# Reordering the loads and folds of the start, and the softmax sums of four slots, in a sparse-attention plus feed-forward kernel

## The chip, the cores and the metric

The kernel runs on one core of a Trainium2 chip. The metric is the device time of one execution in microseconds (us). The core has five engines that run side by side, each with its own instruction queue worked in order: PE (TensorE, matrix products and transposes), DVE (VectorE), ACT (ScalarE), POOL (GpSimd) and SP (SyncE, which here only issues DMAs). POOL issues DMAs as well; its transfers can convert fp32 to fp16 on the way. All transfers share 16 DMA engines.

## The reference

For 8 batches of 8 heads, 576 positions and head size 64, attention is computed under a sparse mask; heads 0 to 3 see the last 32 positions, heads 4 to 7 see the earlier positions with the same remainder modulo 32. The result, 4608 tokens of 512 features, goes through a multiplicative feed-forward layer.

```python
mask_local = (rel >= 0) & (rel < stride)
mask_strided = (rel >= 0) & (pos[None, :] % stride == pos[:, None] % stride)
...
scores = scores - np.max(scores, axis=-1, keepdims=True)
attn = np.exp(scores)
attn = attn / (np.sum(attn, axis=-1, keepdims=True) + 1e-09)
return np.matmul(attn, v).astype(np.float32)
...
a = x @ w1
b = x @ w2
h = a * b @ w3
return (h @ w_out).astype(np.float32)
```

Here w1 and w2 are 512x1024, w3 is 1024x1024 and w_out is 1024x512.

## The kernel before

The attention is cut into 32 pairs of heads, four to a batch: pairs 0 and 1 of a batch are local, 2 and 3 strided. Pair i goes through these steps, each a function:

- `load_qk(i)`: POOL issues the loads of q and k as fp16 into a tile `s16` (four buffers): two DMAs for a local pair, four for a strided one.
- `load_v(i, gate)`: SP issues the loads of v in fp32, three DMAs of 256-byte rows for a local pair (tile `vst`, two buffers) or six for a strided one (tile `vsS`). With `gate` DVE first writes a few zeros into the tile, so that the loads start only when DVE has reached that point in its queue.
- `emit_T`: PE transposes q and k; DVE or ACT copy them out as `qT` and `kT`.
- `emit_S`: PE computes the scores; DVE adds the mask (`tmp`, L312).
- `emit_max` (DVE, L320), `emit_sub` (DVE, L327), `emit_exp` (ACT, L339).
- `emit_norm`: DVE sums a row (`sm`, L347), takes the reciprocal (`rc`, L349), POOL multiplies (L350).
- `emit_cast_v`: v becomes fp16 (`vh`, L260), on POOL, or on ACT for pair 0.
- `emit_P`: PE transposes the probabilities (`pp`), ACT copies them out (`pT`).
- `emit_V`: PE multiplies with v; ACT, and for a strided pair DVE too, write the result into `xT`, the input of the feed-forward layer.

The two last weight matrices are first folded into one: the product of w3 and w_out is computed in eight parts. `fold_t(mc, eng)` transposes a part of w3 on PE (`w3tp`) and copies it out (`w3T`) with DVE (`cp`) or ACT (`act`); `fold_m(mc)` is eight 512-column matrix products with w_out (`fps`, L222) and a copy by ACT (`wfh`, L224). `load_w3(g)` loads the quarter of w3 that folds 2g and 2g+1 take; `load_wo` loads w_out and `load_w12(half)` half of the columns of w1 and w2; all are POOL's.

The feed-forward layer runs in pieces: `emit_a` (four 512-column products `aps`, a copy `asb` by ACT), `emit_b` (four products `bps`, a multiplication `abt` by DVE, L244) and `emit_out` (eight products `ops` with the folded weights, a copy `osb` by ACT, a store by SP). `feed(us, batches)` emits the next pieces in their order until their nominal time, 0.87 us for an a or b piece and twice that for an out piece, has used up a credit; it takes only tokens of the first `batches` batches, so the first piece needs all four pairs of batch 0.

The order is written out by hand: instructions enter each engine's queue in the order of the calls. Loads, folds and the pairs 0 to 4 come one by one (L444 to L537). Then come four slots, n = 5 to 8 (L540 to L561), each with the scores of pair n, the normalisation of pair n-1, the transposes of pair n+1 and some pieces, and then slots n from 9 on with another fixed order (L562 to L590). A strided pair's tiles `vsS`, `qTS` and `prS` exist twice, so pairs use them in turn.

Of the kernel before, what the change touches and what calls it, by code (L numbers as in the profile page):

```python
# [27 lines left out]
def kernel(  # L28
# [49 lines left out]
    def load_qk(i):  # L78

        b, hp, local, par = where(i)  # L80
        h0 = 2 * hp
        t = ld.tile([P, 2, ST * D], FP16, tag="s16", bufs=4, name="s16")
        if i + 1 == 4 * B:
            for p0 in (0, HALF):
                nc.vector.memset(t[p0 + 32:p0 + HALF, :, (ST - 1) * D:ST * D], 0.0)
        for src, p0 in ((q, 0), (k, HALF)):
            if local:
                nc.gpsimd.dma_start(t[p0:p0 + HALF, :, 0:LB * D],
                                    src[b, h0:h0 + 2].rearrange("h (p j) d -> p h (j d)", j=LB))
            elif i + 1 == 4 * B:  # L90
                for r in range(3):
                    n = ST if r < 2 else ST - 1
                    nc.gpsimd.dma_start(t[p0 + NA * r:p0 + NA * r + NA, :, 0:n * D],
                                        _ap(src[b, h0], 11 * r * D,
                                            [[NR * D, NA], [S * D, 2], [1, n * D]]))
            else:
                for h in range(2):
                    nc.gpsimd.dma_start(t[p0:p0 + SW, h, :],  # L98
                                        _ap(src[b, h0 + h], 0,
                                            [[11 * D, 3], [NR * D, NA], [1, ST * D]]))  # L100
        cast[i] = t

    def load_v(i, gate=False):

        b, hp, local, par = where(i)
        h0 = 2 * hp
        if local:
            vt = ld.tile([LW, LB, 2, D], FP32, tag="vL", name="vst")
            if gate:
                nc.vector.memset(vt[:, 0:2, :, 0:1], 0.0)  # L110
            nc.sync.dma_start(vt[:, 0], v[b, h0:h0 + 2, 0:LW].rearrange("h p d -> p h d"))
            for h in range(2):
                nc.sync.dma_start(vt[:, 1:LB, h, :],
                                  _ap(v[b, h0 + h], 32 * D,
                                      [[D, LW], [HALF * D, LB - 1], [1, D]]))
        else:
            vt = vsS[par]
            if gate:
                nc.vector.memset(vt[:, :, 0:1], 0.0)
            for r in range(3):  # L120
                for half in range(2):
                    n = 6 if half == 0 else 5 if r < 2 else 4
                    p0 = HALF * half + NA * r
                    nc.sync.dma_start(vt[p0:p0 + NA, :, 0:n * D],
                                      _ap(v[b, h0], (11 * r + 6 * half) * D,
                                          [[NR * D, NA], [S * D, 2], [1, n * D]]))
        staged[i] = vt
# [70 lines left out]
    def load_w3(g):  # L198
        w3 = wst.tile([P, 2, DF], FP16, tag="w3s", bufs=4, name="w3s")
        nc.gpsimd.dma_start(w3, w3r[:, 2 * g:2 * g + 2, :])  # L200
        for i in range(2):
            w3st[2 * g + i] = w3[:, i, :]
# [5 lines left out]
    def fold_t(mc, eng=nc.vector.tensor_copy):  # L208

        w3 = w3st.pop(mc)  # L210
        tp = psF.tile([P, KC2, P], FP16, tag="f", name="w3tp")
        for kc in range(KC2):
            nc.tensor.transpose(tp[:, kc, :], w3[:, kc * P:(kc + 1) * P], id16)
        w3T = wst.tile([P, KC2, P], FP16, tag="w3T", name="w3T")
        eng(out=w3T, in_=tp)
        aqs[mc] = w3T

    def fold_m(mc):
        w3T = aqs.pop(mc)
        ps = psF.tile([P, DM], FP32, tag="f", name="fps")  # L220
        for kc in range(KC2):
            nc.tensor.matmul(ps, w3T[:, kc, :], woh[:, kc, :], start=(kc == 0),  # L222
                             stop=(kc == KC2 - 1))
        nc.scalar.copy(out=wfh[:, mc, :], in_=ps)  # L224
# [31 lines left out]
    def emit_cast_v(i, eng=nc.gpsimd.tensor_copy):  # L256
        b, hp, local, par = where(i)
        vst = staged.pop(i)
        vh = att.tile(list(vst.shape), FP16, tag="vhL" if local else "vhS", name="vh")
        eng(out=vh, in_=vst)  # L260
        pts[i] = [vh if local else vh.rearrange("p h (t d) -> p t h d", d=D)]
# [180 lines left out]
    cp, act = nc.vector.tensor_copy, nc.scalar.copy  # L442
    with tc.manual_schedule():
        load_qk(0)  # L444
        load_v(0)
        make_identity(nc, id16)
        load_wo()
        make_maskL()
        load_w3(0)
        load_qk(1)  # L450
        load_w3(1)
        for t in qTS + prS:
            nc.vector.memset(t, 0.0)
        make_sel()
        load_qk(2)
        emit_T(0)
        emit_S(0)
        emit_max(0)
        load_v(1, True)
        emit_sub(0)  # L460
        make_maskS()
        emit_exp(0)
        emit_cast_v(0, act)
        for t in vsS:
            nc.vector.memset(t, 0.0)
        load_v(2)
        load_v(3)
        emit_norm(0)
        load_w3(2)
        load_qk(3)  # L470
        load_w3(3)
        load_qk(4)

        fold_t(0, cp)
        emit_T(1)
        fold_t(1, act)
        fold_m(0)
        emit_S(1)
        emit_max(1)
        emit_P(0)  # L480
        emit_sub(1)
        fold_m(1)
        emit_exp(1)
        emit_V(0)
        fold_t(2, cp)
        emit_T(2)
        emit_norm(1)
        fold_m(2)
        emit_S(2)
        emit_max(2)  # L490
        load_w12(0)
        emit_cast_v(1)
        load_qk(5)
        fold_t(3, act)
        emit_sub(2)
        emit_exp(2)
        fold_m(3)
        emit_T(3)
        fold_t(4, act)
        emit_P(1)  # L500
        emit_S(3)
        emit_max(3)
        emit_cast_v(2)
        load_w12(1)
        fold_m(4)
        emit_norm(2)
        emit_sub(3)
        emit_V(1)
        fold_t(5, cp)
        emit_exp(3)  # L510
        fold_t(6, act)
        emit_P(2)
        emit_norm(3)
        emit_cast_v(3)
        load_v(4, True)
        load_qk(6)
        load_qk(7)
        load_qk(8)
        fold_m(5)
        emit_V(2)  # L520
        emit_P(3)
        fold_m(6)
        emit_V(3)
        emit_T(4)
        fold_t(7, cp)
        feed(0.8, 1)
        emit_S(4)
        emit_max(4)
        fold_m(7)
        load_v(5, True)  # L530
        emit_sub(4)
        emit_exp(4)
        load_v(6, True)
        load_v(7)
        feed(1.6, 1)
        emit_T(5)
        feed(1.6, 1)  # L537

        f = 3.6
        for n in range(5, 9):  # L540
            emit_S(n)
            feed(0.15 * f, 1)
            emit_max(n)
            if n > 5:
                emit_V(n - 2)
            feed(0.25 * f, 1)
            emit_norm(n - 1)
            emit_cast_v(n - 1)
            load_qk(n + 4)
            if n > 5:  # L550
                load_v(n + 2)
            emit_sub(n)
            emit_exp(n)
            emit_T(n + 1)
            feed(0.6 * f, 1)
            emit_P(n - 1)
            if n == 8:
                emit_norm(n)
                for i in (8, 9):
                    emit_cast_v(i)  # L560
                load_v(11)  # L561
        for n in range(9, NP + 2):  # L562
            full = (n - 1) // 4
            first = full - 1 if n % 4 == 1 else full
            f = 5.2
            if n + 4 < NP:
                load_qk(n + 4)
            if n + 3 < NP:
                load_v(n + 3)
            if n < NP:  # L570
                emit_S(n)
            emit_V(n - 2)
            if n + 1 < NP:
                emit_T(n + 1)
            feed(0.1 * f, first)
            if n < NP:
                emit_max(n)
            feed(0.15 * f, first)
            if n < NP:
                emit_sub(n)  # L580
                emit_exp(n)
            feed(0.15 * f, full)
            if n <= NP:
                emit_P(n - 1)
            feed(0.2 * f, full)
            if n < NP:
                emit_norm(n)
                if n + 1 < NP:
                    emit_cast_v(n + 1)
            feed(0.4 * f, full)  # L590
        feed(1e9, B)
# [31 lines left out]
```

## Time and profile before

The times are 297.69, 298.36 and 299.65 us, median 298.36. The profiled execution took 297.85 us, of which its span, from the first to the last instruction, is 296.1; 1.75 us lie around it.

| engine | busy us | share of the span | instructions |
|---|---|---|---|
| PE (matrix products) | 268.4 | 91% | 3793 |
| DVE | 192.6 | 65% | 334 |
| ACT | 169.0 | 57% | 297 |
| POOL | 145.9 | 49% | 187 |

HBM is read with 41.43 MB and written with 9.44 MB. On the chain of work that ended last PE has 71% of the span, DVE 10%, ACT 5%, DMA 5%, POOL 4%. Busy time is time in which an engine had an instruction running; matrix products are pipelined, so a busy PE need not be at its peak. "Idle before, releaser" in a row is how long the engine had waited and for whom. Rows of a timeline give start, duration, engine, source line, operation, what it writes and reads, and the idle time before it.

### The profile page before, as it was taken

To read this page: it belongs to the slowest core of one execution; us is meant where nothing else is said; L and a number is where in the kernel's file an instruction comes from. 1 tells how busy PE (TensorE), PEld (TensorE's weight loads), DVE (VectorE), ACT (ScalarE), POOL (GpSimd) and SP (SyncE) were. 2 spreads that over 40 slices of the span, in tenths; PEclk is the share of its full clock that TensorE was granted. 3 is DMA by queue.
4 is the path that set the end of the run, shared out by engine and by line. 5 is a ranking of instruction groups with operands and counts; after the bars stand their busy time and mean duration, and the time that the engine had idled before them with its cause. 6 is when DMAs were issued, how large, how long until landed. Compare 5 with 4: busy or idle time off the path is not lost.

```text
span 296.1 us, 9087 instructions
## 1 busy us (share of the span) xinstructions
PE 268.4 (91%) x3793; PEld 143.6 (48%) x3793; DVE 192.6 (65%) x334; ACT 169.0 (57%) x297; POOL 145.9 (49%) x187
## 2 busy tenths in 40 slices
PE   1179889689799999999999999999999999999994
PEld 0145455345445555555555555555556544444441
DVE  1838647865888778887879787778877870332210
ACT  3326675366656766675676567667667644333322
POOL 8664974368767636873584566456724410000000
PEclk9999999999979999999999999999999999999999
DMA  7999999866689649765965687668613002000113
GB/s 133 187 203 212 192 205 183 158 116 102 143 182 202 101 84 210 124 103 151 194 98 83 181 169 104 117 159 156 122 41 110 2 2 106 35 2 35 71 43 135
DMA packets 65545, 36.70 MB, mean 124 GB/s; under 512 B 45792, under 2 KB 59872, under 8 KB 65504
## 3 DMA queue, kind: packets, MB, share of 16 engines
q0 software_dynamic: 27584, 14.88, 35.9%
q1 hardware_dynamic: 37920, 21.24, 26.7%
q8 instruction: 29, 0.48, 0.7%
q14 instruction: 12, 0.10, 0.1%
HBM read 41.43 MB, written 9.44 MB: 172 GB/s over the span
## 4 chain that ended last, share of the span: by engine, by line
PE 71%; DVE 10%; ACT 5%; DMA 5%; POOL 4%; issue 2%; SPq 1%; DVEq 0%; POOLq 0%; ACTq 0%
PE bps L241 19%; PE ops L249 18%; PE aps L231 17%; PE fps L222 4%; PE sp L306 4%; DMA s<-in_k_dram 4%; DVE tmp L312 3%; DVE mx L320 2%; PE pp L362 2%; PE tpq L272 2%; DVE tmp L327 2%; PE pp L367 2%; PE op L382 2%; DMA vsS<-in_v_dram 2%; ACT pT L363 1%
## 5 line engine op out<-in xcount | busy, mean ns | idle before, releaser
L244 DVE TENSOR_TENSOR abt<-bps,asb 128x512 f16<-128x512 f32 x72 | 49.6, 690 | 39.5 <-PE bps L241 35.2
L241 PE MATMUL bps<-xT,w2h 128*128 128x512 f16 x288 | 74.1, 380 | 0.0
L231 PE MATMUL aps<-xT,w1h 128*128 128x512 f16 x288 | 74.0, 379 | 0.0
L249 PE MATMUL ops<-wfh,abt 128*128 128x512 f16 x288 | 68.3, 386 | 0.0
L235 ACT COPY asb<-aps 128x512 f32<-128x512 f32 x72 | 41.8, 589 | 30.0 <-PE aps L231 29.8
L350 POOL TENSOR_TENSOR pr<-pr,rc 128x864 f16<-128x864 f16 x16 | 27.0, 1690 | 53.4 <-DVE rc L349 29.2
L249 PEld LDWEIGHTS <-abt 128*128 128x128 f16 x288 | 27.5, 99 | 31.5 <-issue 1.6
L252 ACT COPY osb<-ops 128x512 f32<-128x512 f32 x36 | 21.1, 587 | 37.4 <-PE ops L249 34.8
L241 PEld LDWEIGHTS <-w2h 128*128 128x128 f16 x288 | 26.5, 98 | 30.1
L231 PEld LDWEIGHTS <-w1h 128*128 128x128 f16 x288 | 26.9, 98 | 28.3
L350 POOL TENSOR_TENSOR prS<-prS,rc 128x594 f16<-128x594 f16 x16 | 20.1, 1257 | 32.0 <-DVE rc L349 12.1
L327 DVE TENSOR_TENSOR tmp<-tmp,mx 128x864 f32<-128x864 f32 (+1 forms) x32 | 30.6, 957 | 0.9
L320 DVE TENSOR_REDUCE mx<-tmp 128x9 f32<-128x864 f32 (+1 forms) x32 | 29.0, 906 | 0.3
L347 DVE TENSOR_REDUCE sm<-pr 128x9 f32<-128x864 f16 x16 | 16.8, 1049 | 12.8 <-ACT pr L339 12.8
L312 DVE TENSOR_TENSOR tmp<-sp,maskL 128x480 f32<-128x480 f32 (+1 forms) x32 | 18.0, 603 | 9.8 <-PE sp L306 8.9
L339 ACT ACTIVATE pr<-tmp 128x864 f16<-128x864 f32 x16 | 14.8, 923 | 15.9 <-DVE tmp L327 15.1
L272 PE MATMUL tpq<-id,s 54*64 54x54 f16 (+1 forms) x640 | 17.8, 195 | 5.4 <-POOL maskL L140 5.4
L98 POOL DMA_DIRECT2D s<-in_k_dram x30 | 18.0, 612 | 7.0 <-DMA w2h<-in_moe_w_dram 2.7
L272 PEld LDWEIGHTS <-s 54*64 54x64 f16 (+1 forms) x1280 | 14.7, 109 | 10.5 <-DMA s<-in_q_dram 6.5
L272 PE MATMUL tpk<-id,s 54*64 54x54 f16 (+1 forms) x640 | 17.8, 196 | 1.6 <-DMA s<-in_k_dram 1.6
L98 POOL DMA_DIRECT2D s<-in_q_dram x30 | 19.1, 645 | 0.0
L363 ACT COPY pT<-pp 96x640 f16<-96x640 f16 (+1 forms) x32 | 18.6, 630 | 0.6 <-PE pp L362 0.6
(70 smaller groups left out, 334.3 us busy)
## 6 DMA issues: line engine op xcount, KB each, us to landing
out_dram<-osb SPq DMA_DIRECT2D x36, 256.0 KB
vst<-in_v_dram SPq DMA_DIRECT2D x32, 192.0 KB
vsS<-in_v_dram SPq DMA_DIRECT2D x48, 54.0 KB
s<-in_q_dram POOLq DMA_DIRECT2D x16, 144.0 KB, 4.3
s<-in_k_dram POOLq DMA_DIRECT2D x16, 144.0 KB, 5.4
s<-in_q_dram POOLq DMA_DIRECT2D x30, 74.2 KB, 5.8
s<-in_k_dram POOLq DMA_DIRECT2D x30, 74.2 KB, 6.2
w3s<-in_moe_w_dram POOLq DMA_DIRECT2D x4, 512.0 KB, 10.7
```

What stands on the lines that cost most here:

```text
L98: nc.gpsimd.dma_start(t[p0:p0 + SW, h, :], _ap(src[b, h0 + h], 0, [[11 * D, 3], [NR * D, NA], [1, ST * D]]))
L231: nc.tensor.matmul(aps, w1h[:, ci, jc * P:(jc + 1) * P], xT[ci][:, c * NT:(c + 1) * NT], start=(ci == 0), stop=(ci == KC1 - 1))
L235: nc.scalar.copy(out=asb, in_=aps)
L241: nc.tensor.matmul(bps, w2h[:, ci, jc * P:(jc + 1) * P], xT[ci][:, c * NT:(c + 1) * NT], start=(ci == 0), stop=(ci == KC1 - 1))
L244: nc.vector.tensor_mul(abts[c][:, jc, :], bps, abts.pop((c, jc)))
L249: nc.tensor.matmul(ps, abts[c][:, jc, ts * P:(ts + 1) * P], wfh[:, jc, :], start=(jc == 0), stop=(jc == KC2 - 1))
L272: nc.tensor.transpose(tp[HALF * h:HALF * h + HALF, s, :], s16[p0:p0 + npar, h, s * D:(s + 1) * D], id16[p0:p0 + npar, p0:p0 + npar])
L312: nc.vector.tensor_tensor(out=tmp[:, t0:t1, :], in0=sp, in1=msk, op=ALU.add)
L320: nc.vector.tensor_reduce(out=mx, in_=tmp, axis=AX.X, op=ALU.max)
L327: nc.vector.tensor_tensor(out=tmp, in0=tmp, in1=_sub(mx, 0, P, 0, [[1, nt], [0, w]]), op=ALU.subtract)
L350: nc.gpsimd.tensor_tensor(out=prv, in0=prv, in1=_sub(rc, 0, P, 0, [[1, nt], [0, w]]), op=ALU.mult)
L363: nc.scalar.copy(out=pT[:, t0:t1, :], in_=pp)
```

## The change

Only the order of calls changes; no function and no amount of work does.

- Loads of v. Pair 0's load was the second step of the program; now it stands after the maximum of pair 0, gated, where pair 1's stood. Pair 1's moves after the maximum of pair 1, and those of pairs 2 and 3, which stood ungated after the exponential of pair 0, after the maximum of pair 2, both gated.
- Pair 0's v is cast by ACT after the second `fold_t` and no longer right behind the exponential of pair 0.
- Loads of POOL. The first half of w1 and w2 moves ahead of the last quarter of w3. Pair 4's q and k go behind the cast of pair 1, pair 5's and the second half of w1 and w2 behind the normalisation of pair 2.
- `fold_t(6)` moves behind `emit_P(3)`, `fold_m(6)` behind `emit_V(3)`; the first feed-forward piece now precedes `emit_T(4)`, and the second and third pieces stand elsewhere between the steps of pair 4.
- In slots 5 to 8 the sum, reciprocal and normalisation of pair n-1, its cast of v and a load of q and k move ahead of the first piece and of the maximum of pair n; `emit_V(n - 2)` moves behind the second call of `feed`.

```diff
         load_qk(0)
-        load_v(0)
...
         emit_max(0)
-        load_v(1, True)
+        load_v(0, True)
...
         emit_exp(0)
-        emit_cast_v(0, act)
...
-        load_v(2)
-        load_v(3)
         emit_norm(0)
         load_w3(2)
         load_qk(3)
+        load_w12(0)
         load_w3(3)
-        load_qk(4)
 
         fold_t(0, cp)
         emit_T(1)
         fold_t(1, act)
+        emit_cast_v(0, act)
         fold_m(0)
         emit_S(1)
         emit_max(1)
+        load_v(1, True)
         emit_P(0)
...
         emit_max(2)
-        load_w12(0)
+        load_v(2, True)
+        load_v(3, True)
         emit_cast_v(1)
-        load_qk(5)
+        load_qk(4)
...
         emit_cast_v(2)
-        load_w12(1)
         fold_m(4)
         emit_norm(2)
+        load_qk(5)
+        load_w12(1)
         emit_sub(3)
         emit_V(1)
         fold_t(5, cp)
         emit_exp(3)
-        fold_t(6, act)
         emit_P(2)
         emit_norm(3)
         emit_cast_v(3)
...
         emit_V(2)
         emit_P(3)
+        fold_t(6, act)
+        emit_V(3)
         fold_m(6)
-        emit_V(3)
-        emit_T(4)
         fold_t(7, cp)
         feed(0.8, 1)
+        emit_T(4)
+        fold_m(7)
         emit_S(4)
         emit_max(4)
-        fold_m(7)
+        feed(0.8, 1)
         load_v(5, True)
         emit_sub(4)
         emit_exp(4)
         load_v(6, True)
         load_v(7)
-        feed(1.6, 1)
+        feed(0.8, 1)
         emit_T(5)
         feed(1.6, 1)
...
         for n in range(5, 9):
             emit_S(n)
-            feed(0.15 * f, 1)
-            emit_max(n)
-            if n > 5:
-                emit_V(n - 2)
-            feed(0.25 * f, 1)
             emit_norm(n - 1)
             emit_cast_v(n - 1)
             load_qk(n + 4)
+            feed(0.15 * f, 1)
+            emit_max(n)
+            feed(0.25 * f, 1)
             if n > 5:
+                emit_V(n - 2)
                 load_v(n + 2)
             emit_sub(n)
             emit_exp(n)
```

## The prediction

> **What bounds the kernel now.** I read the busy times by stretch first, then what PE waited for, then the timeline where those waits lie. Stretches (start and end, length, then busy us of PE, its weight loads, DVE, ACT, POOL; granted clock, DMA share, GB/s):
>
> ```profile
> 16.00:24.00 8.00, 6.99 (x91) 4.52 (x92) 2.82 (x5) 3.07 (x5) 5.44 (x7) 1.00 1.18 207
> 24.00:32.00 8.00, 6.52 (x120) 3.62 (x118) 6.90 (x10) 4.60 (x8) 4.78 (x7) 1.00 1.10 200
> ...
> 56.00:64.00 8.00, 5.67 (x110) 3.04 (x109) 5.83 (x11) 4.41 (x8) 4.54 (x4) 1.00 0.54 116
> ...
> 80.00:88.00 8.00, 7.26 (x115) 4.05 (x115) 6.40 (x10) 4.76 (x9) 6.52 (x8) 0.79 0.78 174
> 88.00:120.00 32.00, 32.00 (x546) 17.72 (x544) 25.47 (x46) 22.01 (x42) 19.06 (x23) 1.00 0.78 157
> ```
>
> From 88 us on PE never rests and the order is unchanged, so whatever is won or lost by then stays to the end. Until about 56 us the DMA engines are full (share above 1); from 56 to 82 PE idles though DMA is not full. What PE waited for between 16 and 90 us (sum, times, longest):
>
> ```profile
> PE w3tp L213 <- DMA w3s<-in_moe_w_dram: 3.8, 1, 3.8
> PE pp L362 <- POOL pr L350: 3.6, 2, 2.3
> PE op L395 <- ACT pT L370: 1.2, 2, 0.6
> PE fps L222 <- ACT w3T L215: 1.2, 1, 1.2
> ```
>
> The second and third rows lie in slots 5 to 8. One of these waits in the timeline (slot 6; start, duration, engine):
>
> ```profile
> 60.35 0.84 DVE L312 TENSOR_TENSOR tmp<-sp,maskS 128x324 f32<-128x324 f32 x2 [1.61 <-PE sp L306]
> 61.55 0.69 DVE L244 TENSOR_TENSOR abt<-bps,asb 128x512 f16<-128x512 f32 x1 [0.35 <-PE bps L241]
> 62.15 0.76 DVE L320 TENSOR_REDUCE mx<-tmp 128x11 f32<-128x594 f32 x1
> 62.83 1.04 DVE L347 TENSOR_REDUCE sm<-pr 128x9 f32<-128x864 f16 x1
> ...
> 64.35 1.97 POOL L350 TENSOR_TENSOR pr<-pr,rc 128x864 f16<-128x864 f16 x1 [2.80 <-DVE rc L349]
> ...
> 66.37 0.70 PE L362 MATMUL pp<-id,pr 128*96 128x128 f16 x9 [1.26 <-POOL pr L350]
> ```
>
> The sum of pair 5 stands behind a piece's multiplication and the maximum of pair 6, though its exponential ended at 58.8. The loop sum, POOL, transpose, scores, mask, sum takes 7.06 us (the transposes of pairs 4 and 5 start at 59.31 and 66.37).
>
> **Sums first (slots 5 to 8).** The sum can start when `tmp` ends, at 61.2 and not 62.83: 1.6 us off the loop. What limits next: PE's own work in a slot is scores 0.5, transposes 0.5 and 0.65, the product with v 0.42 and about 4.1 pieces of 0.87, 5.65 us together. DVE's is, in slot 5 with local pairs, 1.12 + 1.05 + 0.25 + 2 x 0.69 + 1.05 + 1.06 + 0.46 = 6.4; in slot 6, where pair 6 is strided, about 5.5. The maximum now waits behind sum and reciprocal (1.3), so the exponential comes 1.3 later; its next reader, the sum of the following slot, starts about 2 us after it now (58.8 to 61.2), so this is covered, barely in slot 6. I take 5.45, 6.05, 5.5 and 5.5 us for the slots: 22.5 between the scores of pairs 5 and 9, which now stand at 52.28 and 80.62, 28.34 apart. Gain 5.8; at least 0 if DVE becomes the loop, at most 6.3 (all PE's idle from 56 to 80, 2.33 + 1.26 + 1.52, and 1.2 of the waits for `pT`). The later product with v costs PE nothing: a piece stands in its place while ACT copies `pT`.
>
> **The clock.** In 79.0 to 82.4 PE runs only transposes and small products, and the next eight 512-column products run at half clock:
>
> ```profile
> 79.00:82.40 3.40, 1.81 (x91) 1.55 (x90) 2.58 (x5) 2.91 (x6) 3.40 (x5) 1.00 0.75 179
> 82.40:85.90 3.50, 3.50 (x25) 1.33 (x18) 3.47 (x5) 0.98 (x2) 3.50 (x4) 0.51 0.85 206
> ```
>
> They take 3.53 us where the eight before took 1.90. With the slots closed up that gap falls to about 2.4 us, shorter than any that led to half clock here: gain 1.65 (0 if it comes anyway).
>
> **The start.** Without pair 0's v the first loads are alone. Pair 0's q (issued at 1.34) and k landed at 5.38 and 6.72; a q issued at 60.31 among little traffic landed 3.43 us later. So k of pair 0 lands near 5.6 and all behind it 1.1 us earlier: the first w3 quarter at 15.4 instead of 16.49, pair 1's k at 17.1 instead of 18.19. (Bounds 0 and 1.9, the time that v's packets took, 31 us over 16 engines.) The scores of pair 0 gain nearly nothing: ACT copies kT only behind the mask, at 7.5.
>
> **Pair 0's v.** It now starts where pair 1's did, about 11.1. Pair 1's, issued from 11.29, landed at 25.2 by its completion events: while POOL's loads were queued, the packets of the two queues went one for one (1,103 and 1,112 between 18.5 and 22.0), and v has 1,728. With POOL's queue 1.1 us ahead I take 24.4; the lower bound is 18, by the 6.9 us from 60.38 to 67.2 with little beside. ACT waits for it in front of `wfh`, `pT` of pair 0 and the exponential of pair 1. Its queue: cast 1.14 to 25.6, `wfh` 0.59, `pT` 1.17 to 27.3. `fold_m(1)` ends on PE at 24.0 (25.1 less 1.1); the product with v of pair 0 ends at 27.5 instead of 25.5: 2.0 late, a PE gap of 2.7.
>
> **Pairs 1 to 3.** Pair 1's v, issued at 23.7 behind its maximum, gets the same one-for-one share and lands near 34; POOL waits for it (free at 31.8), and behind its cast stand pair 4's loads, the cast of pair 2 and the normalisation of pair 2. Pair 2's v is issued from 32.7 to 34.8 and follows it through SP's rings: near 39 (the DMAs of a strided v took 6 us under load before, and 3 us free). Cast 0.82, multiplication 1.5: 41.4, where it ended at 39.16. Then, new in this place, four issues on POOL (two of 0.61, two of 0.78: 2.8 us) before pair 3 is normalised: 45.4 instead of 41.3. The last transpose of batch 0 starts at 45.45 instead of 41.69.
>
> **Folds and first piece.** `fold_t(6)` fills the wait for `pT`. But its copy follows `pT` on ACT (0.8, then 1.0), so `fold_m(6)` runs from 47.85 to 49.6; with `fold_t(7)` the first piece is at 50.15, now 44.95. Moving w1/w2's half forward brings nothing: it lands at 41.0 already, before the first piece can run. Moving the last w3 quarter back costs nothing: 34.5 becomes about 40, and its fold is due at 46. The same holds for what POOL issues later: pair 4's loads (from 35) land near 42 and are due at 51, pair 5's near 46, due at 55, the second half of w1/w2 (from 42.6) near 51, due with the ninth piece after 60. The added gate writes are 0.06 us each on DVE. The shuffled pieces around pair 4 are neutral: same work on PE. From there to the scores of pair 5 it is 7.33 us now (with the transposes of pair 4 ahead): 57.6 instead of 52.28, **5.3 late**; POOL's six loads are done by 53, before the sum of pair 4.
>
> **Sum.** +5.3 - 5.8 - 1.65 = -2.15 against 297.85 (span 296.1 and 1.75 around it). For half clock in the new gaps (next) I add 0.8, one time in two of 1.65: -1.35, 296.5. The median of the runs lies 0.5 above the profiled one: **297.0**.
>
> **A rule against it.** The rows say that 3.4 us with hardly a 512-column product are followed by half clock. The change makes two such gaps at the start: 24.0 to 28.9 and 43.6 to 47.85, 4.9 and 4.2 us. Both followed by it costs 3.3 instead of 0.8. The Trainium skill, page "TensorE: Matmul & The Clock Gate" (Part 1), says that the clock halves after an idle window of 3413 ns whose phase runs free of the kernel; the records here agree with the length, 3.41 us, and by it a 4.9 us gap would hold a whole window less than half of the time.
>
> **Rivals.**
> 1. *Loads of v land sooner* than I take, near the unloaded bounds (nothing else of SP's is queued with them). For: unloaded v lands in 2 to 7 us. Against: POOL's ring is full until 40. Then ACT and POOL don't wait; POOL's 2.8 us of issues and the fold behind `pT` remain, the scores of pair 5 are 2.0 late: 2.0 - 5.8 - 1.65 = -5.45, 292.9 as a median.
> 2. *Both gaps at half clock*: -2.15 + 3.3 = +1.15, 299.5.
> 3. *Slower: POOL behind pair 2's v.* If it takes from 32.7 as long as pair 4's, issued at 40.09 and landed at 51.66, it lands at 44.3, 5 us later, and everything to the first piece shifts by that: -1.35 + 5 = +3.65, 302.0. It decides from a landing of about 41.5 on.
>
> That the early half of w1/w2 does nothing is in the forecast already.
>
> **Chances.** Forecast 0.40 (a fifth of it below 295.4), rival 1 0.26, rival 2 0.10, rival 3 0.24. A measurement can tell about 1% (3 us) from no change. Faster 0.26 + 0.08 = 0.34; within 1% 0.32 + 0.10 = 0.42; slower 0.24. Range 292.5 to 302.5 takes in both ends; the likeliest case alone has 295 to 299.
>
> **What would show it.** Right: a PE gap near 24 to 27 released by ACT; `fps` of fold 6 behind a POOL wait near 45; scores of pair 5 near 57 and of pair 9 near 79.5; no half clock near 82. Wrong: first piece before 47 (rival 1), pair 2's cast after 42 (rival 3), or slots that still take 7 us with DVE releasing PE.

## The result and the profile after

The changed kernel took 306.61 us (median of four runs, 305.01 to 307.69) against 299.0 us for the kernel before on the same chip (median of four): a ratio of 1.027, 95% interval 1.022 to 1.031. The change makes the kernel 2.7% slower. The profiled execution after took 305.01 us, its span is 303.3; before it was 297.85 and 296.1, so the two profiles differ by 7.2 us. The page's head and engine totals after:

```profile
span 303.3 us, 9092 instructions
PE 270.3 (89%) x3793; PEld 144.9 (48%) x3793; DVE 192.8 (64%) x337; ACT 168.1 (55%) x297; POOL 145.4 (48%) x187
```

PE has the same 3793 instructions and 1.9 us more busy time (268.4 before); the other 5.3 us are idle time. Where it lies is read from the start of each pair's scores on PE (L306), of the first feed-forward piece (L231) and of the transposes of pair 2's and pair 3's probabilities (L367). Each row is a stretch between two such starts, so the last column can be added up:

| stretch on PE | before, us | after, us | predicted | measured |
|---|---|---|---|---|
| start to the scores of pair 3 | 34.43 | 36.75 | +2.0 | +2.32 |
| to the transposes of pair 2's probabilities | 4.79 | 5.96 | +0.24 | +1.17 |
| to those of pair 3 | 2.47 | 3.92 | +1.52 | +1.45 |
| to the first piece | 3.26 | 4.76 | +1.44 | +1.50 |
| to the scores of pair 5 | 7.33 | 10.05 | +0.1 | +2.72 |
| four slots, to the scores of pair 9 | 28.34 | 27.96 | -5.8 | -0.38 |
| to the scores of pair 10 | 9.31 | 7.67 | -1.65 | -1.64 |
| new half clock, as an allowance | | | +0.8 | in the rows above |
| sum | | | -1.35 | +7.14 |

From the scores of pair 10 to the end both profiles run alike: every later start is 7.14 us later. The busy times by stretch, with the columns as before (length; busy us of PE, weight loads, DVE, ACT, POOL; granted clock, DMA share, GB/s):

```profile
16.00:24.00 8.00, 7.44 (x86) 4.42 (x87) 1.95 (x3) 1.65 (x2) 5.92 (x8) 1.00 1.19 206
...
40.00:48.00 8.00, 5.43 (x58) 3.11 (x59) 2.60 (x7) 3.53 (x7) 8.00 (x12) 0.79 0.87 149
...
80.00:88.00 8.00, 6.95 (x105) 3.40 (x104) 5.42 (x10) 4.57 (x8) 5.14 (x7) 1.00 0.71 135
88.00:120.00 32.00, 30.47 (x542) 17.32 (x542) 25.95 (x46) 22.59 (x41) 20.84 (x25) 1.00 0.73 154
```

The low granted clock has left the row from 80 to 88 (0.79 before, 1.00 now) and stands in the row from 40 to 48, where POOL is busy throughout. What stands ahead of half clock before, a gap with transposes and small products alone, is still there, now near 88 us, but the clock stays at 1.00:

```profile
88.40:92.00 3.60, 2.47 (x94) 1.88 (x94) 3.32 (x8) 3.11 (x6) 2.94 (x4) 1.00 0.90 192
```

From 87.31 to 91.29, 3.98 us, PE has no 512-column product (3.36 us before, from 79.16 to 82.52), and yet the next eight, from 91.29 on, take 1.90 us. In 88 to 120, where PE never rested before, it now lacks 1.5 us: the last slots end later. What PE waited for from 16 to 98 us (sum, times, longest):

```profile
...
PE pp L367 <- POOL prS L350: 2.4, 2, 2.2
PE sp L306 <- ACT kT L281: 2.2, 1, 2.2
PE pp L367 <- ACT qT L281: 1.9, 2, 1.6
...
PE pp L362 <- DVE qTS L285: 1.6, 2, 1.3
PE pp L362 <- ACT kT L286: 1.3, 2, 0.7
```

The largest row of the slots before, `pp` behind POOL's `pr` (3.6 us), is gone. In its place stand rows of about the same sum whose releasers are the copies `qT`, `qTS` and `kT` of the next pair (1.9 less 0.9 that was there before, 1.6 and 1.3). Slot 5 shows why (start, duration, engine, source line):

```profile
64.43 1.63 POOL L350 TENSOR_TENSOR pr<-pr,rc 128x864 f16<-128x864 f16 x1 [6.47 <-DMA vsS<-in_v_dram]
...
65.85 1.12 DVE L327 TENSOR_TENSOR tmp<-tmp,mx 128x864 f32<-128x864 f32 x1
...
66.89 0.45 DVE L285 COPY qTS<-tpq 128x594 f16<-128x594 f16 x1
67.06 0.92 ACT L339 ACTIVATE pr<-tmp 128x864 f16<-128x864 f32 x1 [2.60 <-DVE tmp L327]
...
67.40 0.44 PE L362 MATMUL pp<-id,pr 128*96 128x128 f16 x5 [1.26 <-DVE qTS L285]
67.89 0.64 ACT L286 COPY kT<-tpk 128x594 f16<-128x594 f16 x1
...
68.58 0.38 PE L362 MATMUL pp<-id,pr 128*96 128x128 f16 x4 [0.74 <-ACT kT L286]
68.89 0.53 PE L306 MATMUL sp<-kT,qTS 64*64 64x54 f16 x22
```

POOL's multiplication, which PE used to wait for, is done at 66.06. Yet the transposes of `pr` start at 67.40 and their second half at 68.58. They write into the same two PSUM buffers (PSUM is the memory that PE writes into; the pool `psA` has two buffers) as `tpq` and `tpk`, the transposes of the next pair, and these come free when DVE has copied `qTS` and ACT has copied `kT`. Those copies stand behind the subtraction and the exponential of pair 5 in their engines' queues. The scores of pair 6 read both copies. Before, the same chain ran in slot 5, at the same pace:

```profile
57.00 2.25 POOL L350 TENSOR_TENSOR pr<-pr,rc 128x864 f16<-128x864 f16 x1 [5.34 <-DMA vsS<-in_v_dram]
...
58.69 0.64 ACT L286 COPY kT<-tpk 128x594 f16<-128x594 f16 x1
...
59.31 0.70 PE L362 MATMUL pp<-id,pr 128*96 128x128 f16 x9 [2.33 <-POOL pr L350]
```

There `pr` ended at 59.25 and `kT` at 59.33: two paths of equal length, of which the waits name one. From the scores to the exponential it was 52.28 to 57.86, 5.58 us; now it is 61.44 to 67.06, 5.62. The sum and the reciprocal were ahead of the subtraction already; exchanging them with the maximum moves nothing behind the subtraction.

At the start, POOL's queue (start, duration) shows the chain that delays pairs 2 and 3:

```profile
38.32 1.14 POOL L260 CAST vh<-vst 96x1152 f16<-96x1152 f32 x1 [5.87 <-DMA vst<-in_v_dram]
...
41.47 1.19 POOL L350 TENSOR_TENSOR prS<-prS,rc 128x594 f16<-128x594 f16 x1
...
45.35 1.22 POOL L350 TENSOR_TENSOR prS<-prS,rc 128x594 f16<-128x594 f16 x1
```

POOL stood 5.87 us for the v of pair 1, landed at 38.17; the v of pair 2, at 39.50, was no longer waited for. And PE's queue there:

```profile
42.71 0.51 PE L367 MATMUL pp<-id,prS 128*128 128x128 f16 x6 [2.17 <-POOL prS L350]
43.06 2.88 PE L222 MATMUL fps<-woh,w3T 128*128 128x512 f16 x8
...
46.63 0.77 PE L367 MATMUL pp<-id,prS 128*128 128x128 f16 x6 [0.24 <-POOL prS L350]
```

Fold 5 took 2.88 us here and 1.89 before: it lies in a stretch of half clock.

### The profile page after: what moved, and what is told of

It is laid out like the page before. It is cut to its first block, busy times and chain, and to the rows that moved or that the text cites. A ratio compares the mean times of both kernels' runs of the same rounds, so it can differ in the third digit from the quotient of the medians.

```text
span 303.3 us, 9092 instructions
## 1 busy us (share of the span) xinstructions
PE 270.3 (89%) x3793; PEld 144.9 (48%) x3793; DVE 192.8 (64%) x337; ACT 168.1 (55%) x297; POOL 145.4 (48%) x187
## 4 chain that ended last, share of the span: by engine, by line
PE 67%; DVE 13%; ACT 8%; DMA 4%; POOL 3%; issue 3%; SPq 0%; POOLq 0%; ACTq 0%; DVEq 0%
PE bps L241 18%; PE ops L249 17%; PE aps L231 17%; DMA vst<-in_v_dram 4%; PE sp L306 4%; DVE tmp L312 3%; DVE mx L320 3%; DVE tmp L327 3%; PE fps L222 2%; PE tpq L272 2%; PE pp L362 2%; ACT pT L363 2%; PE op L382 2%; PE pp L367 2%; ACT pr L339 1%
## 5 line engine op out<-in xcount | busy, mean ns | idle before, releaser
L231 PE MATMUL aps<-xT,w1h 128*128 128x512 f16 x288 | 74.0, 379 | 0.0
L249 PE MATMUL ops<-wfh,abt 128*128 128x512 f16 x288 | 66.8, 380 | 0.0
L350 POOL TENSOR_TENSOR pr<-pr,rc 128x864 f16<-128x864 f16 x16 | 26.0, 1625 | 58.2 <-DVE rc L349 32.8
L231 PEld LDWEIGHTS <-w1h 128*128 128x128 f16 x288 | 27.1, 98 | 28.7
L350 POOL TENSOR_TENSOR prS<-prS,rc 128x594 f16<-128x594 f16 x16 | 18.9, 1180 | 29.4 <-ACT asb L235 13.1
L260 POOL CAST vh<-vst 96x1152 f16<-96x1152 f32 x15 | 18.3, 1225 | 5.9 <-DMA vst<-in_v_dram 5.9
L222 PE MATMUL fps<-woh,w3T 128*128 128x512 f16 x64 | 17.9, 430 | 2.1 <-ACT w3T L215 1.7
```

Of the source, the lines that this page charges most:

```text
L231: nc.tensor.matmul(aps, w1h[:, ci, jc * P:(jc + 1) * P], xT[ci][:, c * NT:(c + 1) * NT], start=(ci == 0), stop=(ci == KC1 - 1))
L249: nc.tensor.matmul(ps, abts[c][:, jc, ts * P:(ts + 1) * P], wfh[:, jc, :], start=(jc == 0), stop=(jc == KC2 - 1))
L350: nc.gpsimd.tensor_tensor(out=prv, in0=prv, in1=_sub(rc, 0, P, 0, [[1, nt], [0, w]]), op=ALU.mult)
```

## The experiments

The theory after this reading: (a) the slots gain nothing because the copies of the next pair's q and k are a second path of the same length; (b) the fold that was between the scores of pair 4 and the pieces was a cover, and taking it away costs about 2.2 us; (c) the loads of v, held back, cost the rest through ACT (pair 0) and POOL (pairs 1 and 2), with POOL's new issues. The rivals are named in each expectation. Times are medians, ratios are against the kernel before on the same chip in the same set. One caution for the profiles: with identical code ahead of it, the scores of pair 5 start at 52.04 to 53.70 us in the profiles of before and of the four kernels that change the slots alone. The spread is there at the scores of pair 3 already: 34.19 to 35.86 in six profiles with the old start. So stretches inside one profile are compared, and whole times by their medians.

### The slots

**The new slots alone, on the kernel before.** (In the cuts of the slots some lines are joined by semicolons.)

```diff
         for n in range(5, 9):
             emit_S(n)
-            feed(0.15 * f, 1); emit_max(n)
-            if n > 5: emit_V(n - 2)
-            feed(0.25 * f, 1)
             emit_norm(n - 1); emit_cast_v(n - 1); load_qk(n + 4)
-            if n > 5: load_v(n + 2)
+            feed(0.15 * f, 1); emit_max(n); feed(0.25 * f, 1)
+            if n > 5: emit_V(n - 2); load_v(n + 2)
```

> The kernel before with the new slots 5 to 8 alone. Theory (copies): the next scores wait for the copies of the next pair's q and k, which stand on DVE behind the subtraction and on ACT behind the exponential; before and after, mask, maximum, sum, reciprocal and subtraction all stand ahead of them, only sum and maximum are swapped. Then the scores of pairs 5 to 9 keep their distance of 28.3 us (27.5 to 28.5) and the time is that of before within 1 us; half clock near 82 may or may not stay (1.6 us). Rival (the prediction): 22.5 us between these scores and 5 to 7 us less in time, and then the loss of 7.6 us must come from a start that alone costs 13.

Measured: 296.85 us against 298.05, ratio 0.994 (0.990 to 0.997). The four slots take 27.98 us, as in the whole change, and the half clock after them is gone (granted clock 1.00, 9.31 becomes 7.67 us to the scores of pair 10). What PE waited for (30 to 98 us):

```profile
PE pp L362 <- ACT kT L286: 2.2, 3, 0.9
PE pp L367 <- ACT qT L281: 1.9, 2, 1.6
PE pp L362 <- DVE qTS L285: 1.6, 2, 1.3
```

The three copies are the releasers again. The predicted gain of 5.8 us is not lost to the changes of the start: it isn't there.

**The same, with the transposes of the next pair ahead of the maximum.**

```diff
-            feed(0.15 * f, 1); emit_max(n); feed(0.25 * f, 1)
+            feed(0.15 * f, 1); emit_T(n + 1); emit_max(n); feed(0.25 * f, 1)
...
-            emit_T(n + 1)
```

> The kernel before with the new slots, and in them also the transposes of pair n+1 ahead of the maximum of pair n, so that the copies of q and k no longer stand behind subtraction and exponential. Theory (copies): the loop that held the slots is cut, and the sum, now early, pays: about 23 to 25 us between the scores of pairs 5 and 9, no half clock near 82, 4 to 7 us less than before. Rival (DVE or POOL is the loop by its own work, some 6.4 us in a slot): 26 us or more, at most 2 us less than before. Prediction's view: the transposes' place is indifferent, so the same as the new slots alone.

Measured: 296.13 us, ratio 0.990 (0.986 to 0.993). Slot 5 falls to 5.30 us, slot 6 rises to 9.65, the four take 27.07. The hoped-for gain was missed, because of a wait that the expectation did not have:

```profile
PE tpq L272 <- ACT pT L363: 2.0, 1, 2.0
```

The transposes now come before ACT has emptied the two PSUM buffers of the probabilities before (`pT`). A stretch of half clock followed in slot 6, from 63.3 to 66.7. The theory holds in slot 5 and the place of the transposes was wrong.

**The transposes between the second piece and the product with v, ahead of the subtraction.** Beside it, in the same set, this move alone with the old order of sum and maximum.

```diff
             feed(0.25 * f, 1)
+            emit_T(n + 1)
             if n > 5: emit_V(n - 2); load_v(n + 2)
             emit_sub(n); emit_exp(n)
-            emit_T(n + 1)
```

> The kernel before with the new slots and the transposes of pair n+1 between the second call of feed and the product with v of pair n-2, so that the copies of q and k stand ahead of subtraction and exponential but the transposes no longer wait long for the PSUM buffers that ACT empties for the pair before. Theory (copies, and two PSUM buffers): no PE wait above 1 us for a transpose in slot 6, 24 to 26.5 us between the scores of pairs 5 and 9, 3 to 5 us below before. Rival (DVE's own work and its slower subtractions beside POOL hold the slots): 26.5 to 28 us, at most 2.5 us below before.

> The kernel before, its slots in their old order but with the transposes of pair n+1 ahead of the subtraction of pair n. Theory: both paths must be cut; with the sum behind the maximum POOL's normalisation still ends 6.9 us after the scores, so the slots keep 26.5 to 28.5 us and the time is within 1.5 us of before. Rival (the copies alone hold the slots): as with the sums first, 3 us or more below before.

Measured: with the new slots 294.18 us against 298.66, ratio 0.983 (0.980 to 0.986), lower than both kernels of this case; the slots take 24.11 us. The transposes alone give 297.08 us, ratio 0.994 (0.991 to 0.997), and slots of 27.37 us, with PE behind POOL's `pr` again (1.7 us once, the row that the kernel before has). So there are two paths of nearly equal length: each edit alone cuts one and gains 1.2 to 1.6 us, and both together gain 4.5. In the slots themselves that is 0.36 and 0.97 us against 4.23; the rest of the two small gains can come from half clock behind the slots, which the profile of before has and these two lack. Slot 5 of the faster kernel:

```profile
56.36 0.66 ACT L286 COPY kT<-tpk 128x594 f16<-128x594 f16 x1
56.38 1.63 POOL L350 TENSOR_TENSOR pr<-pr,rc 128x864 f16<-128x864 f16 x1 [5.35 <-DVE rc L349]
...
58.06 1.96 DVE L327 TENSOR_TENSOR tmp<-tmp,mx 128x864 f32<-128x864 f32 x1
58.07 0.70 PE L362 MATMUL pp<-id,pr 128*96 128x128 f16 x9
```

`kT` is copied at 56.36, before the subtraction, and the transposes of `pr` start as POOL ends, with no wait. One wait of 1.1 us of a transpose for `pT` was left in slot 6, just above what the expectation allowed.

### The loads of v

**The loads of v 0 to 3 held back and the cast of pair 0 moved, on the kernel before.**

```diff
-        load_v(0)
...
-        load_v(1, True)
+        load_v(0, True)
...
-        emit_cast_v(0, act)
...
-        load_v(2)
-        load_v(3)
...
+        emit_cast_v(0, act)
...
         emit_max(1)
+        load_v(1, True)
...
         emit_max(2)
+        load_v(2, True)
+        load_v(3, True)
```

> The kernel before with the loads of v of pairs 0 to 3 and the cast of pair 0 as after, all else as before. Theory (ACT waits for v of pair 0, POOL for v of pair 1 and 2): the product with v of pair 0 ends 2 us later, scores of pair 3 are 2.0 to 2.5 us late, the first piece 3 to 4.5 us, and the time rises by 3 to 5 us, less what half clock near 82 gives or takes (1.6). Rival (the loads of POOL in their new order are what delays pairs 2 and 3): first piece at most 2.5 us late, time up by 1 to 2.5 us.

Measured: 308.1 us against 298.05, ratio 1.032 (1.027 to 1.036). That is twice what was expected and at least as slow as the whole change; the first piece starts at 53.89, 8.9 us late where 3 to 4.5 were expected. POOL's queue there:

```profile
42.33 0.82 POOL L260 CAST vh<-vsS 128x768 f16<-128x768 f32 x1 [5.51 <-DMA vsS<-in_v_dram]
```

Here the v of pair 2 shares the DMA engines with the first half of w1 and w2, which POOL issued just before (32.83), and lands at 42.0. POOL waits 5.51 us for it, PE 4.85 for POOL's normalisation behind it (45.89), and two stretches of half clock follow (44.0 to 50.8; fold 5 takes 3.62). This is the third rival of the prediction, in a kernel that lacks the early half of w1 and w2. The v of pair 1, on the other hand, comes sooner than in the whole change: issued at 26.07, it lands at 34.36.

**The same for pair 0's v alone** (the v of pair 1 then follows ungated, those of pairs 2 and 3 stay).

> The kernel before with pair 0's v alone held back (loaded after the maximum of pair 0, pair 1's right behind it, pairs 2 and 3 ungated as before) and its cast by ACT behind fold 1's transposes. Theory (two stalls add up in the loads of v: ACT for pair 0, 2 us, and POOL for pairs 1 and 2, the rest): the product with v of pair 0 and the scores of pair 3 are 2 to 2.7 us late, the first piece 2 to 3, and the time is 1 to 4 us above before, well below the 9.8 us of all four loads. Rival (ACT's stall alone starts the whole loss, since everything behind it on PE, DVE and POOL shifts and meets half clock): 6 us or more above before.

Measured: 301.3 us against 298.51, ratio 1.011 (1.006 to 1.015). The product with v of pair 0 starts at 27.61 here and at 27.01 in the kernel after; before it had ended at 25.5. The time is as the theory has it, the profile is not: the scores of pair 3 start at 38.95 and the first piece at 49.47, both 4.5 us late where 2 to 3 were expected. It is of one of the two longest of the seven runs (303.62 us) and has three stretches of half clock where the profile of before has one; the first lies in the fold behind that product (3.30 us where 1.90 is usual).

**The whole change without its edits on v.**

```diff
+        load_v(0)
...
-        load_v(0, True)
+        load_v(1, True)
...
+        emit_cast_v(0, act)
...
+        load_v(2)
+        load_v(3)
...
-        emit_cast_v(0, act)
...
-        load_v(1, True)
...
-        load_v(2, True)
-        load_v(3, True)
```

> The changed kernel with the loads of v of pairs 0 to 3 and the cast of pair 0 where they were before. Theory (the held-back loads are the main loss): scores of pair 3 at 34 to 35.5, first piece at 46 to 48.5, PE's wait for kT of pair 5 (2.2 us) stays, and the time is 300 to 303.5, 3 to 6.5 us below the changed kernel. Rival (POOL's issues between the normalisations of pairs 2 and 3, and the folds' order, are the main loss): 304 or more.

Measured: 303.14 us against 298.51, ratio 1.017 (1.013 to 1.022). Without the loads of v the other parts cost 4.6 us; the edits on v add some 3 us to that, though alone they cost 10. The first piece starts at 48.41 us (44.95 before, 51.39 after).

### POOL's issues

**The issues of pair 5's q and k and of the second half of w1 and w2 moved behind the cast of pair 3's v, in the kernel after.**

```diff
         emit_norm(2)
-        load_qk(5)
-        load_w12(1)
...
         emit_norm(3)
         emit_cast_v(3)
+        load_qk(5)
+        load_w12(1)
```

> The kernel after, with pair 5's q and k and the second half of w1 and w2 issued behind the cast of pair 3's v, so that POOL normalises pair 3 right behind pair 2. Theory (the issues cost less than their 2.8 us, because PE has a fold and a product with v to do meanwhile): the last transpose of batch 0 follows the one before it by 2.5 us (3.5 where that fold is at half clock), not by 3.92; the first piece 0.4 to 1.4 us sooner; 305 to 306.5 us. Rival (the prediction's step taken at its full price): first piece 2.8 us sooner, about 303.8 us. Second rival (the loads, issued later, come too late for the pieces): slower than the kernel after, and PE shows a wait for w1h, w2h or pair 5's transposes.

Measured: 305.82 us against 299.17, ratio 1.022 (1.015 to 1.029); the kernel after stood at 306.61. POOL normalises pairs 2 and 3 in one go, and PE's queue reads:

```profile
43.29 0.51 PE L367 MATMUL pp<-id,prS 128*128 128x128 f16 x6 [2.17 <-POOL prS L350]
...
46.91 0.82 PE L367 MATMUL pp<-id,prS 128*128 128x128 f16 x6
```

The time is within the theory's range, but not clear of that of the kernel after, and the first piece, at 51.73, is not sooner (51.39; from the transposes of pair 2 on it is 8.44 us for 8.68). From transposes to transposes it is 3.62 us without any wait, where it was 3.92 with one of 0.24. In the changed kernel the 2.8 us of issues thus cost 0.3: the fold and the product with v, at half clock, cover the rest (2.90 and 0.52 us here). In the kernel without the edits on v, where that fold ran in 1.89 us, the wait was 1.40. The full price of 2.8 is shown in neither.

**The same loads issued earlier: pairs 4 and 5 and the second half of w1 and w2 ahead of the cast of pair 1's v, in the kernel after.**

```diff
+        load_qk(4)
+        load_qk(5)
+        load_w12(1)
         emit_cast_v(1)
-        load_qk(4)
...
-        load_qk(5)
-        load_w12(1)
```

> The changed kernel with the loads of pairs 4 and 5 and of the second half of w1 and w2 issued by POOL ahead of the cast of pair 1, while POOL waits for that v, and not behind the cast and the normalisation of pair 2. Theory (POOL's 4 us of issues stand in the path of pairs 2 and 3): normalisation of pair 3 3 to 4 us earlier, first piece at 48 to 49, time 2 to 4 us below the changed kernel. Rival (the transfers then meet the loads of v of pairs 1 to 3, whose packets share the DMA engines one for one): v of pair 2 lands after 42 and not at 39.5, and the time is the same or up to 3 us above.

Measured: 309.78 us against 298.51, ratio 1.040 (1.032 to 1.047), some 3 us above the kernel after. Its v of pair 1 lands at 41.74 instead of 38.17, that of pair 2 at 42.61 instead of 39.50, and PE waits for the cast:

```profile
PE op L382 <- POOL vh L260: 3.7, 1, 3.7
```

More bulk in POOL's queue delays what SP's queue brings; the rival is right. Part of the 3 us can be the clock: this profile has half clock from 41.5 to 48.3 and from 72.2 to 75.6.

**The first half of w1 and w2 ahead of the last quarter of w3, alone, on the kernel before.**

```diff
         load_w3(2)
         load_qk(3)
+        load_w12(0)
         load_w3(3)
...
-        load_w12(0)
```

> The kernel before with one thing moved: the first half of w1 and w2 issued ahead of the last quarter of w3. Theory (the early half does nothing): 297.5 to 299.5 us, the half lands near 36 instead of 41 and nobody waits for it in either place; the last quarter of w3 lands some 2 to 4 us later. Rival: that quarter, needed at about 37.8 us here, comes too late, PE waits for it at the transposes of fold 6, and the first piece is 1 to 3 us later: 300 to 301.5 us.

Measured: 299.12 us against 299.17, ratio 1.000 (0.997 to 1.004): no effect, as the prediction had it, though the quarter of w3 lands at 39.56 instead of 34.46. PE does not wait for it in this profile, but the profile is of the slowest of the ten runs: a subtraction of 4.20 us on DVE (0.78 in the kernel after) delays PE ahead of it, and the transposes of folds 5 and 6 start at 40.86.

### The folds and pieces around pair 4

**These alone, on the kernel before.**

```diff
-        fold_t(6, act)
         emit_P(2)
...
         emit_P(3)
+        fold_t(6, act)
+        emit_V(3)
         fold_m(6)
-        emit_V(3)
-        emit_T(4)
         fold_t(7, cp)
         feed(0.8, 1)
+        emit_T(4)
+        fold_m(7)
         emit_S(4)
         emit_max(4)
-        fold_m(7)
+        feed(0.8, 1)
...
-        feed(1.6, 1)
+        feed(0.8, 1)
         emit_T(5)
```

> The kernel before with the folds 6 and 7 and the pieces around pair 4 as after, all else as before. Theory (lost cover): with fold 7 ahead of the scores of pair 4, PE has little to do between those scores and the scores of pair 5, whose kT stands on ACT behind the exponential of pair 4; a PE wait for kT of about 2 us appears ahead of the scores of pair 5, and the time rises by 2 to 3.5 us. Rival (the prediction: shuffled pieces and folds are neutral): within 1 us of before, scores of pair 5 at 52 to 53.

Measured: 302.13 us against 298.05, ratio 1.010 (1.006 to 1.015). The first piece starts at 46.45, 1.5 us later than in the profile of before, and the scores of pair 5 come 10.05 us after it (7.33 before), with this wait:

```profile
PE sp L306 <- ACT kT L281: 2.2, 1, 2.2
```

**The kernel after, with fold 7 and the pieces around pair 4 in the old order.** (`fold_m(7)` back behind the maximum of pair 4, `emit_T(4)` back ahead of `fold_t(7)`, the two pieces joined again.)

> The changed kernel with fold 7, the pieces and the transposes around pair 4 in the order of before (fold 6 stays behind batch 0). Theory (lost cover): the 2.2 us wait for kT ahead of the scores of pair 5 is gone and from the first piece to these scores it is 7.3 us again and not 10; 2 to 3.5 us below the changed kernel. Rival (pair 5 is late anyway, PE waits elsewhere): within 1 us of the changed kernel.

Measured: 306.15 us against 298.51, ratio 1.028 (1.022 to 1.032), no different from the kernel after. In its profile the wait for `kT` is gone and the stretch from the first piece to the scores of pair 5 is back at 7.33 us; but that profile also has three stretches of half clock (near 30, 50 and 91 us; the kernel after has one), enough to take back what it won. The mechanism is confirmed by the stretch, its effect on the time of the changed kernel is open.

## Why the prediction was wrong

The prediction gave 297.0 us, within 292.5 to 302.5; the kernel takes 306.6. Two steps failed and make up 8.0 of the 8.5 us between the predicted and the measured sum; the landing of pair 1's v was too early, the start gained less than assumed, and one number was right by luck.

- **What limits the slots next: failed, 5.4 us.** The step priced PE's and DVE's work in a slot and asked who next reads the exponential. It did not ask what stands behind the exponential in ACT's queue (`kT` of the next pair) and behind the subtraction in DVE's (`qTS`), nor that PE's transposes share two PSUM buffers with these copies. The new slots alone show 27.98 us instead of 22.5, released by these copies. Its statement that the exponential comes 1.3 us later was wrong too: 5.58 and 5.62 us after the scores. That PE stopped waiting for POOL was right, and worth nothing by itself.
- **"The shuffled pieces around pair 4 are neutral": failed, 2.7 us.** PE's work is the same, but `fold_m(7)` filled the time in which the scores of pair 4 went through mask, maximum, subtraction and exponential. Ahead of the scores it covers nothing: ACT copies `kT` of pair 5 behind that exponential at 60.74, and PE stands 2.21 us. The row of 2.2 appears in the folds alone and goes when the old order is put back.
- **Pair 1's v: too early by 4 us, worth about 1.2.** Predicted near 34, it landed at 38.17: issued 2 us later than assumed and 12.4 us on the way instead of 10.3. That it kept POOL from pair 2 was in the text; pair 2's normalisation ended at 42.66 and not 41.4. The likely cause of the longer way is a term that the prediction put at nothing: in the whole change POOL issues the early half of w1 and w2 at 22.65, ahead of this v. With the edits on v alone that half is issued at 32.83, behind it, and the v is 8.3 us on the way. The place of pair 4's loads differs too, so this is not shown by itself.
- **The start: 0.4 to 0.5 us gained, not 1.1.** The first transposes of w3 start at 16.00 instead of 16.53, those of pair 1's k at 17.86 instead of 18.24. Then the first fold took 3.62 us (2.54 before; in all profiles it takes between these), so that the scores of pair 1 came 0.70 us later than before. This is most of why pair 1's v was issued late.
- **Pair 0's v: right in the chain.** 24.64 for 24.4; ACT's cast from 24.74 to 25.9, `pT` to 27.45 for 27.3. PE itself came later than assumed and waited 1.03 us instead of 2.7, but ACT's end decides. That the scores of pair 3 are 2.3 late for 2.0 is in part luck: identical code puts them anywhere from 34.19 to 35.86 with the old start (six profiles) and from 36.75 to 39.13 with the new one (three).
- **Pair 2's v and the third rival.** It landed at 39.50 for 39, below the 41.5 from which that rival decides. So the rival had the right sign, about half of the size (302.0 for 306.6 us), and not the cause. It does decide in the kernel with the edits on v alone (42.0).
- **The four issues on POOL: the sum right, by another way.** The stretch between the two transposes grew by 1.45 us for a predicted 1.5. But the issues cost 0.3 of it in this kernel, half clock in fold 5 (2.88 for 1.89 us) 1.0.
- **Fold 6 behind `pT`: right,** 1.50 us for 1.4. **The early half of w1 and w2:** alone without effect, as said. In the whole change it probably helps the v of pair 2 (39.50, against 42.0 where POOL issues that half just ahead of it) and delays that of pair 1; this was not tried by itself.
- **The clock: the number near 82 right (1.64 for 1.65 us), by luck.** The step expected the gap ahead of it to fall to 2.4 us because the slots close up. The slots did not close up, the gap grew to 3.98 us, and half clock stayed away all the same. It does not go by the slots: with the edits on v alone, which keep the old slots, a gap of 3.35 us was not followed by it (1.90 us for the eight products); in the whole change without its edits on v, which has the new slots, one of 4.10 us was (3.33 us). The new stretch, 43.8 to 47.2, follows neither of the two named gaps but 3.85 us without a 512-column product from 39.21 to 43.06; both named places have one in the profile of the changed kernel with the old order around pair 4 (near 30 and 50 us). Of the four runs of the kernel after, two have a granted clock of 0.994 (305.0 and 306.2 us) and two of 0.989 (307.0 and 307.7).

The parts do not add up: in medians v alone costs 10.1 us, the folds and pieces 4.1, the slots gain 1.2, and all the rest without v costs 4.6, while the whole change costs 7.6. The moved loads of POOL keep w1 and w2 out of the way of pair 2's v and put them into that of pair 1; how much of the difference is theirs stays open.

## What to carry to other kernels

When a wait is taken away, look for the second chain that ends at the same time: follow what is queued behind each instruction of the loop on its own engine, and who shares its PSUM buffers, not only who reads its result; with two chains of nearly equal length each edit alone is worth little, and both together were worth 4.5 us. Independent work between a step and its long way through other engines is a cover, and moving it is not neutral because the amount of work is the same. A load that is held back to make room must be priced with the queues that wait for it in order: here POOL stood 5.9 us behind the v of pair 1.

## What the hardware showed

- **Half clock comes and goes between runs of one kernel.** Ten runs of the new slots alone have a granted clock of 1.000 or 0.994, the four of the kernel with the edits on v alone 0.975 to 0.988. A stretch is 3.4 us long. The Trainium skill, page "TensorE: Matmul & The Clock Gate" (Part 1), gives an idle window of 3413 ns that runs free of the kernel; the length and the changing places agree. PE was not idle in it, though: in that gap of the kernel before (79.0 to 82.4) it was busy for 1.81 of 3.40 us, with small products alone. And such a gap is a chance and no rule: 3.36 and 4.10 us were followed by half clock, 3.35 and 3.98 us were not. A fold of eight products that falls into a stretch, wholly or in part, takes 2.88 to 3.62 us instead of 1.90.
- **DVE and POOL stop each other.** In slot 5 after, the subtraction starts at 65.85 and takes 1.12 us, and the cast on POOL, begun at 66.01, takes 1.96 instead of 1.13. In the fastest kernel the cast begins first, at 57.97, and takes 1.13, and the subtraction, from 58.06, takes 1.96. In these two rows whoever comes second waits for about the rest of the first. The Trainium skill, page "SBUF — State Buffer" (Summary: rules for kernel authors), says that where DVE has two SBUF inputs while a GpSimd instruction reads SBUF, the second to issue blocks until the first finishes; these two rows agree. A third is less plain: with the new slots alone the subtraction of pair 2, from 31.10, takes 2.63 us where the kernel after takes 0.78, although the cast on POOL beside it begins later, at 31.92, and takes 1.17; POOL had been issuing DMAs since 30.36. Such rows, and the first fold, make up part of the spread between profiles of identical code.
- **A small transfer behind bulk.** The 432 KB of pair 1's v, 256 bytes to a row, took 12.4 us from issue to landing while POOL's loads were queued, 15.6 with more of them (26.19 to 41.74) and 8.3 with fewer (26.07 to 34.36).
